# Another order for the first 24 units of a Fourier transform fused with a feed-forward layer

## The chip, the cores and the metric

The kernel runs on one core of a Trainium2 chip. The metric is the device time of one execution in microseconds (us); smaller is better. The core's engines work side by side, each through its own list of instructions in order: TensorE (PE in the profile, with its weight loads as PEld), VectorE (DVE), ScalarE (ACT), GpSimd (POOL) and SyncE (SP), which issues most DMA transfers. An engine waits only where an instruction needs another engine's or a transfer's result, or a buffer that is still in use.

## The reference

```python
X = np.fft.fft(x, axis=1)            # x: 8 batches, 3008 positions, 256 channels
X = np.fft.fft(X, axis=2).real       # 24064 tokens of 256
h = X @ w_in                         # w_in: 256 x 2048
g = np.where(h >= 1, h, np.where(h <= -1, 0.0, (h + 1) ** 2 / 4))
return g @ w_out                     # w_out: 2048 x 256
```

The inputs x are float32; w_in and w_out reach the chip as 64-bit floats, which the kernel converts itself by their bit fields.

## The kernel before

**Tiling.** The transform over 3008 = 64 x 47 positions is made in two stages of matmuls. Stage 1 (PE L276, tiles `s1`) takes sums and differences of mirrored positions, which DVE or POOL folds first (`y`, L132); its results are copied to `z` (ACT L299, DVE L297). Stage 2 (PE L342, tiles `s2`) multiplies z by a constant table `rm` and is split by ACT and DVE into a high and a low part, `pqh` and `pql` (L162, L163). One column, the Nyquist channel, takes a way of its own: a small matmul (L315), a copy, a transfer to memory (`nyr`) and transfers back, spread over all partitions (`nyb`).

The transform over channels is folded into w_in: two constant matrices `cm`, cosine and sine, multiply w_in (PE L251, bank `wps`), and the product is split into `wh` (ACT L252) and `wl` (DVE L262). This is done for four blocks of 512 columns; each block is two folds, one per matrix: `f0 f1`, `f2 f3`, `f4 f5`, `f6 f7`, with `s0` to `s7` as the low parts. Row 0 of the sine product belongs to the Nyquist channel: it is copied to `row` (ACT L255), POOL sets that row of wh and wl to zero (L265), and `spread_delta` turns the row into columns of `delta`, one scalar per partition, with four matmuls of one column each (PE L242) and a copy (ACT L243).

**Units.** The feed-forward part runs in units: one block of 128 of the 2048 hidden columns for one chunk of up to 512 positions. `gemm1` is six matmuls (PE L379, banks `uv`, three of them, two per unit), then on DVE `us` (L382, which reads nyb and delta) and two `h` (L384, L385), and on ACT `a` (L388, L389). `activate` makes `g` on DVE (L397). `gemm2`, the second product, adds g times w_out to four accumulator banks (PE L438); after the last unit of a group the banks are copied out (DVE L449, ACT L447) and stored. There are 384 units. The first twelve take columns 0 to 3 of the first batch's three chunks, the next 36 its other columns, so accumulator groups end with units 3, 7, 11, 23 and so on. Units 0 to 23 use w_out unsplit.

**What sets the order.** For units 0 to 23 the instructions are pinned: each engine works in the order in which the program writes them. Lists of steps, START and STEPS, write the rest of the work between: `l` loads weights, `k` and `m` load constants, `x` loads x, `a`, `b`, `c` and `d` or `v` convert one weight block (fields on DVE L196 and L197; floats on ACT L202 to L204; join on DVE L209 and L210; scale on POOL or DVE L224), `y` folds x, `p` issues matmuls of stage 1, Nyquist or stage 2, `z` and `w` copy stage 1, `t` copies its last column, `q` splits stage 2, `o` splits w_out, `f`, `s` and `e` are the folds above. `p0` to `p7` are stage 1, `p8` the Nyquist matmul, `p9` and on stage 2. In each unit of the loop gemm1 comes first, then activate of the unit before, then the steps, then gemm2 of the unit four before (LAG).

Of the kernel before, what the change touches and what calls it, by code (L numbers as in the profile page):

```python
# [110 lines left out]
def fft_ffn_kernel(ctx: ExitStack, tc: tile.TileContext, x, cst, w_in, w_out, out):  # L111
# [124 lines left out]
    folds, deltas = {}, {}  # L236

    def spread_delta(f4):
# [4 lines left out]
        nc.scalar.activation(delta[:, f4 * 4 : f4 * 4 + 4], pt[:, :4], AF.Copy)  # L243


    def fold_w_in(n):
# [5 lines left out]
        nc.scalar.activation(wh[m][:, cols], pt, AF.Copy)  # L252
        if m == 1:
            row = sb.tile([1, CH], F32, tag="us", name=f"row_{f4}", bufs=2)
            nc.scalar.activation(row, pt[0:1], AF.Copy)  # L255
            deltas[f4] = row
        folds[n] = pt

    def fold_low(n):
# [2 lines left out]
        nc.vector.tensor_tensor(wl[m][:, cols], folds.pop(n), wh[m][:, cols].bitcast(F32), op=ALU.subtract)  # L262
# [349 lines left out]
```

## Time and profile before

| | us |
|---|---|
| median of 3 runs | 1776.84 (1775.87 to 1780.36) |
| the profiled execution's own time | 1775.3 |
| its span, first to last instruction | 1773.5 |
| PE busy | 1743.4 (98%) |
| DVE busy | 1424.8 (80%) |
| ACT busy | 1337.5 (75%) |
| POOL busy | 1162.9 (66%) |
| chain of waits, share of PE | 45% |
| mean granted clock of PE | 0.994 |

PE is busy nearly throughout, so the page as a whole shows little; the first 150 us are the part in which PE has idle time, and there the views by stretch, the waits and the rows in order of time are to be read. A row of the timeline has its start, its duration, the engine, the line, the operation and the count of instructions merged in it; in square brackets stands the idle time ahead of it and who ended it. A matmul of 32-bit floats counts as two instructions.

### The profile page before, as it was taken

The page shows a single profiled execution, that of the slowest core. Times are in us where ns is not written, and L with a number is a line of the kernel's source. Part 1 is how long each engine was busy: PE and PEld are TensorE (multiplying, and loading weights), DVE is VectorE, ACT ScalarE, POOL GpSimd, SP SyncE. Part 2 cuts the span into 40 slices and gives each one's busy share as a digit, 9 for nine tenths or more (in the row PEclk, how much of TensorE's full clock was granted, in tenths as well). Part 3 has the DMA queues.
Part 4 walks back from the last instruction along what each step waited for, and adds up shares of the span by engine and source line. Part 5 has one row for each costly group of instructions (what it writes and reads, how often), then busy time and mean ns, then how long its engine had stood idle before and what let it go on. Part 6 is the DMA issues. An engine that isn't in the chain of part 4 may idle for free.

```text
span 1773.5 us, 21522 instructions
## 1 busy us (share of the span) xinstructions
PE 1743.4 (98%) x7826; PEld 1399.5 (79%) x7826; DVE 1424.8 (80%) x1746; ACT 1337.5 (75%) x1567; POOL 1162.9 (66%) x813
## 2 busy tenths in 40 slices
PE   7889999999999999999999999999999999999998
PEld 5445788888888888888888888888888878888876
DVE  5898787888887888878878878877888778888886
ACT  5676777887777877777777877788778787777775
POOL 0113776876677767677667776677666766667776
PEclk9899999999999999999999999999999999999999
DMA  8003321110011100111001100011000000000000
GB/s 311 23 24 129 130 78 44 41 58 19 24 50 45 60 30 1 60 36 58 30 12 61 59 30 25 16 57 59 30 25 36 1 23 30 13 24 8 16 24 24
DMA packets 32010, 80.88 MB, mean 46 GB/s; under 512 B 2976, under 2 KB 8224, under 8 KB 31904
## 3 DMA queue, kind: packets, MB, share of 16 engines
q1 hardware_dynamic: 31868, 79.51, 12.8%
q8 instruction: 61, 1.00, 0.2%
q14 instruction: 45, 0.37, 0.1%
q10 hardware_dynamic: 36, 0.01, 0.0%
HBM read 51.70 MB, written 27.81 MB: 45 GB/s over the span
## 4 chain that ended last, share of the span: by engine, by line
PE 45%; ACT 21%; DVE 13%; POOL 12%; issue 9%; DMA 0%; ACTq 0%; POOLq 0%; SPq 0%; DVEq 0%
PE acc L438 27%; PE uv L379 13%; POOL gl L406 11%; DVE h L400 9%; ACT a L389 7%; ACT gh L403 6%; ACT a L388 5%; PE s L276 2%; PE s L342 1%; DVE h L384 1%; ACT z L299 1%; DVE h L385 1%; PE wps L251 1%; DVE us L382 0%; DMA raw<-in_moe_w_in_dram 0%
## 5 line engine op out<-in xcount | busy, mean ns | idle before, releaser
L406 POOL TENSOR_TENSOR gl<-h,gh 128x512 fp32r<-128x512 f32 (+1 forms) x720 | 1037.8, 1463 | 438.8 <-ACT gh L403 406.9
L400 DVE SCALAR_TENSOR_TENSOR h<-a,h 128x1024 f32<-128x1024 f32 (+1 forms) x360 | 544.8, 1513 | 219.4 <-ACT a L389 217.9
L403 ACT ACTIVATE gh<-h 128x1024 fp32r<-128x1024 f32 (+1 forms) x360 | 376.2, 1045 | 345.2 <-DVE h L400 318.5
L438 PE MATMUL acc<-gh,woh 128*128 128x512 f32 (+1 forms) x1440 | 570.9, 396 | 3.7 <-DVE o L449 2.2
L438 PE MATMUL acc<-gl,woh 128*128 128x512 f32 (+1 forms) x1440 | 564.4, 392 | 0.9 <-POOL gl L406 0.9
L438 PE MATMUL acc<-gh,wol 128*128 128x512 f32 (+1 forms) x1440 | 561.5, 390 | 0.0
L388 ACT ACTIVATE a<-h,biases 128x1024 f32<-128x1024 f32 (+1 forms) x384 | 431.7, 1124 | 36.4 <-DVE h L385 34.5
L389 ACT ACTIVATE a<-a 128x1024 f32<-128x1024 f32 (+1 forms) x384 | 398.9, 1039 | 7.7
L379 PE MATMUL uv<-pqh,wh 128*128 128x512 f32 (+1 forms) x768 | 311.5, 406 | 11.3 <-DVE us L382 8.3
L438 PEld LDWEIGHTS acc<-gh,woh 128*128 128x128 f32 x1440 | 271.2, 188 | 62.0 <-DVE o L449 5.8
L438 PEld LDWEIGHTS acc<-gl,woh 128*128 128x128 f32 x1440 | 271.5, 189 | 58.3 <-POOL gl L406 2.2
L438 PEld LDWEIGHTS acc<-gh,wol 128*128 128x128 f32 x1440 | 271.1, 188 | 54.2
L384 DVE TENSOR_TENSOR h<-us,uv 128x512 f32<-128x512 f32 (+1 forms) x384 | 259.8, 677 | 61.3 <-POOL gl L406 19.1
L382 DVE SCALAR_TENSOR_TENSOR us<-nyb,delta,uv 128x512 f32<-128x512 f32 (+1 forms) x384 | 279.2, 727 | 30.0 <-PE uv L379 29.8
L379 PE MATMUL uv<-pql,wh 128*128 128x512 f32 (+1 forms) x768 | 300.3, 391 | 0.0
L379 PE MATMUL uv<-pqh,wl 128*128 128x512 f32 (+1 forms) x768 | 300.2, 391 | 0.0
L385 DVE TENSOR_TENSOR h<-us,uv 128x512 f32<-128x512 f32 (+1 forms) x384 | 256.4, 668 | 0.0
L379 PEld LDWEIGHTS uv<-pqh,wh 128*128 128x128 f32 x768 | 144.8, 189 | 57.1 <-DVE us L382 13.8
L379 PEld LDWEIGHTS uv<-pqh,wl 128*128 128x128 f32 x768 | 145.0, 189 | 32.6 <-issue 4.7
L379 PEld LDWEIGHTS uv<-pql,wh 128*128 128x128 f32 x768 | 144.9, 189 | 30.4 <-DVE pql L163 0.4
L132 POOL TENSOR_TENSOR y<-x 96x512 f32<-96x512 f32 x56 | 97.9, 1750 | 2.9 <-PE s L276 2.9
L438 PE MATMUL acc<-g,wo 128*128 128x482 f32 (+1 forms) x192 | 85.2, 585 | 5.1 <-DVE o L449 3.9
(59 smaller groups left out, 707.6 us busy)
## 6 DMA issues: line engine op xcount, KB each, us to landing
x<-in_x_dram SPq DMA_DIRECT2D x64, 512.0 KB, 3.4
out_dram<-o SPq DMA_DIRECT2D x26, 512.0 KB, 2.8
out_dram<-o SPq DMA_DIRECT2D x14, 482.0 KB, 2.9
nyb<-nyr SPq DMA_DIRECT2D x24, 256.0 KB, 3.2
raw<-in_moe_w_in_dram SPq DMA_DIRECT2D x4, 512.0 KB, 8.7
raw<-in_moe_w_out_dram SPq DMA_DIRECT2D x4, 512.0 KB, 10.4
part<-o SPq DMA_DIRECT2D x4, 512.0 KB, 2.6
os<-part SPq DMA_DIRECT2D x4, 512.0 KB, 4.4
```

The source lines that it names most:

```text
L132: (engine or nc.gpsimd).tensor_tensor(y, t[:96, 0], t[:96, 1], op=ALU.add)
L276: nc.tensor.matmul(pt[:, i], y[:, i * P : (i + 1) * P], bm[:96, :], start=True, stop=True)
L379: nc.tensor.matmul(t[:, :n], w[m][:, cols], r[:, m, :n], start=(j == 0), stop=(j == 2))
L382: nc.vector.scalar_tensor_tensor(us, nyb[b, k][:, :n], delta[:, f : f + 1], uv[0], op0=ALU.mult, op1=ALU.add)
L384: nc.vector.tensor_tensor(h[:, 0], us, uv[1], op=ALU.subtract)
L385: nc.vector.tensor_tensor(h[:, 1], us, uv[1], op=ALU.add)
L388: nc.scalar.activation(a, h, AF.Relu, bias=half, scale=0.5)
L389: nc.scalar.activation(a, a, AF.Square)
L400: nc.vector.scalar_tensor_tensor(h, a, 1.0, h, op0=ALU.min, op1=ALU.max)
L403: nc.scalar.activation(gh, h, AF.Copy)
L406: nc.gpsimd.tensor_tensor(gl[:, sg], h[:, sg], gh[:, sg].bitcast(F32), op=ALU.subtract)
L438: nc.tensor.matmul(acc[:, :n], w, g[:, sg], start=(begin and j == 0), stop=(last and j == len(terms) - 1))
```

## The change

The diff, cut to its core; the new functions and the lines that changed in the loop are whole.

```diff
+SKIP = (7, 13)
 START = (
-    "l0 k l1 x0 x1 m0 x2 x3 x4 x5 x6 x7 l2 "
-    "a0 b0 a1 b1 c0 v0 y0 p0 t0 c1 y1 z0 v1 p1 p8 n0 l3 l4 l5 n1 n2 l6 l7 l8 l9 l10 l11 l12 l13 l14 l15 "
-    "y2 z1 f0 y3 p2 p3 z2 y4 s0 p4 w3 f1 y5 p5 w4 y6 p6 s1 w5 y7 p7 w6 e0 w7 p9 p10 q9 q10 a2 b2"
+    "l0 l1 k x0 x1 x2 m0 x3 x4 x5 x6 x7 l2 a0 b0 a1 b1 c0 v0 y0 p0 t0 z0 p8 n0 "
+    "l3 l4 l5 n1 n2 l6 l7 l8 l9 l10 l11 l12 l13 l14 l15 c1 v1 f0 y1 p1 z1 y2 s0 f1 p2 y3 z2 y4 p3 s1 y5 w3 p4 "
+    "y6 w4 p5 y7 w5 p6 w6 p7 e0 w7 E0 p9 p10 q9 q10 a2 b2"
 )
 STEPS = {
-    0: "p11 q11 c2 d2",
-    1: "p12 q12 a3 b3",
+    0: "p11 q11 c2 d2 i5",
+    1: "p12 q12 a3 b3 i5",
...
-    7: "f2 f3 c6 d6 s2 s3 a7 b7",
-    8: "e1 c7 d7",
+    7: "f2 f3 c6 d6 s2 s3 r1 a7 b7",
+    8: "c7 d7",
...
-    17: "o3 L",
-    18: "f6 f7 s6 s7 a14 b14",
-    19: "e3 Y0 c14 d14",
+    17: "o3 L a14 b14",
+    18: "f6 f7 s6 s7 r3",
+    19: "Y0 c14 v14",
...
-EARLY_BANKS = 14
+EARLY_BANKS = 12
...
-    for i, v in enumerate((0.5, 1151.0, 255.0 * 2**23, 1.0)):
+    for i, v in enumerate((0.5, 1151.0, 255.0 * 2**23, 1.0, 1.0)):
...
+    nc.vector.memset(inner[0:1], 0.0)
...
+    def copy_delta(f4):
+        nc.scalar.activation(delta[:, f4 * 4 : f4 * 4 + 4], spreads.pop(f4)[:, :4], AF.Copy)
+
+    def move_delta(f4):
+        row = deltas.pop(f4)
+        for i in range(4):
+            nc.sync.dma_start(
+                delta[:, f4 * 4 + i : f4 * 4 + i + 1], row[:, i * P : (i + 1) * P].rearrange("o (p x) -> o p x", x=1)
+            )
...
-        nc.scalar.activation(wh[m][:, cols], pt, AF.Copy)
+        nc.scalar.activation(wh[m][:, cols], pt, AF.Copy, scale=inner if m else 1.0)
...
-        nc.vector.tensor_tensor(wl[m][:, cols], folds.pop(n), wh[m][:, cols].bitcast(F32), op=ALU.subtract)
+        high = wh[m][:, cols].bitcast(F32)
         if m == 1:
-            for t in (wh[1], wl[1]):
-                nc.gpsimd.memset(t[0:1, cols].bitcast(F32), 0.0)
+            nc.vector.scalar_tensor_tensor(wl[m][:, cols], folds.pop(n), inner, high, op0=ALU.mult, op1=ALU.subtract)
+        else:
+            nc.vector.tensor_tensor(wl[m][:, cols], folds.pop(n), high, op=ALU.subtract)
...
+    def keep_warm(n, src):
+        bank = ps.tile([P, CH], F32, tag="acc3", name="warm_bank", bufs=1)[:, : src.shape[1]]
         for _ in range(n):
-            nc.tensor.matmul(warm_bank[:, :width], warm[:, :P], warm[:, :width], start=True, stop=True)
+            nc.tensor.matmul(bank, src[:, :P], src, start=True, stop=True)
...
+        if 2 <= i < PINNED and i not in SKIP:
+            gemm2(second)
+            second += 1
+        if i < n_units:
             run_steps(STEPS.get(i, ""))
-        if i >= LAG and i < PINNED:
-            gemm2(i - LAG)
```

Steps 13 and 14 change as 7 and 8 do: `r2` in unit 13, no `e2` in unit 14.

**Second product.** It starts in unit 2 and lags two units; none is issued in units 7 and 13, so the lag is three from there and four from unit 14 on, as before. Within a unit it now comes before the steps, so the copies of the accumulators come before the unit's conversions.

**Start.** Both folds of the first block of w_in move ahead of most of stage 1; the second weight load goes ahead of the constants, the load of `cm` behind that of x2; the copy of the first delta (`E0`) goes behind the last copies to z.

**Delta.** The first block keeps its four matmuls. The other three are moved by four transfers each from the row to columns of delta (`r1` to `r3`), in the unit of the fold, and their row takes a buffer of `y`. Row 0 of wh and wl becomes zero by a scalar `inner`, 0 in partition 0 and 1 elsewhere, instead of by POOL's memsets.

**Smaller.** Five matmuls of 128 columns (`i5`) in each of units 0 and 1 write a bank that nobody reads; two of stage 2's banks are no longer those of the accumulators; job 14 is converted one unit earlier and scaled on DVE.

Where rows move, first on PE at the start. Before, from the second stage 1 to the first delta:

```order
L276 MATMUL s_0_1_151<-cs,y_1_144 128x96 x4
L315 MATMUL ny_156<-cs,z_133 24x64
L251 MATMUL wps_194<-cv_114,cm 128x512
L251 MATMUL wps_194<-cv_120,cm 128x512
L276 MATMUL s_0_2_200<-cs,y_2_188 128x96 x4
L276 MATMUL s_0_3_205<-cs,y_3_198 128x96 x4
L276 MATMUL s_0_4_217<-cs,y_4_214 128x96 x4
L251 MATMUL wps_226<-cv_114,cm 128x512
L251 MATMUL wps_226<-cv_120,cm 128x512
L276 MATMUL s_0_5_234<-cs,y_5_232 128x96 x4
```

The changed kernel at the same place:

```order
L327 MATMUL ny_148<-cs,z_135 24x64
L262 MATMUL wps_183<-cv_116,cm 128x512
L262 MATMUL wps_183<-cv_122,cm 128x512
L288 MATMUL s_0_1_189<-cs,y_1_187 128x96 x4
L262 MATMUL wps_201<-cv_116,cm 128x512
L262 MATMUL wps_201<-cv_122,cm 128x512
L288 MATMUL s_0_2_207<-cs,y_2_198 128x96 x4
L288 MATMUL s_0_3_220<-cs,y_3_212 128x96 x4
L288 MATMUL s_0_4_232<-cs,y_4_218 128x96 x4
L288 MATMUL s_0_5_243<-cs,y_5_226 128x96 x4
```

The second fold (the second `wps`) moved from behind five blocks of stage 1 to behind two.

Next DVE in unit 15, where an accumulator group ends. Before, from the unit's `g` to the next unit's `us`:

```order
L397 SCALAR_TENSOR_TENSOR g_831<-a_791,h_788 128x2x482
L209 SCALAR_TENSOR_TENSOR cv_805<-raw_180,cv_805 128x512
L210 SCALAR_TENSOR_TENSOR cv_805<-raw_180,cv_805 128x512
L224 TENSOR_TENSOR cv_805<-cv_805 128x512
L196 TENSOR_SCALAR cv_836<-raw_182 128x512
L197 TENSOR_SCALAR cv_836<-raw_182 128x512
L449 COPY o_0_842<-acc_0_726 128x512
L449 COPY o_1_849<-acc_2_728 128x512
L382 SCALAR_TENSOR_TENSOR us_864<-nyb_0_162,delta,uv_0_856 128x482
```

The changed kernel:

```order
L409 SCALAR_TENSOR_TENSOR g_835<-a_801,h_798 128x2x482
L461 COPY o_0_837<-acc_0_699 128x512
L461 COPY o_1_844<-acc_2_701 128x512
L211 SCALAR_TENSOR_TENSOR cv_813<-raw_172,cv_813 128x512
L212 SCALAR_TENSOR_TENSOR cv_813<-raw_172,cv_813 128x512
L226 TENSOR_TENSOR cv_813<-cv_813 128x512
L198 TENSOR_SCALAR cv_854<-raw_174 128x512
L199 TENSOR_SCALAR cv_854<-raw_174 128x512
L394 SCALAR_TENSOR_TENSOR us_868<-nyb_0_154,delta,uv_0_860 128x482
```

The two copies that free accumulator banks moved ahead of the conversion of two weight blocks.

Last PE around the second block's folds (units 7 and 8). The changed kernel, from the last `uv` rows of unit 7:

```order
L391 MATMUL uv_1_547<-pql_1_317,wh_69 128x512
L262 MATMUL wps_561<-cv_423,cm 128x512
L262 MATMUL wps_561<-cv_463,cm 128x512
L262 MATMUL wps_565<-cv_423,cm 128x512
L262 MATMUL wps_565<-cv_463,cm 128x512
L391 MATMUL uv_0_587<-pqh_2_451,wh_68 128x512
L391 MATMUL uv_0_587<-pqh_2_451,wl_70 128x512
L391 MATMUL uv_0_587<-pql_2_452,wh_68 128x512
L391 MATMUL uv_1_591<-pqh_2_451,wh_69 128x512
```

Before, four rows of the second product of unit 3 (`acc`) stood between the last `wps` and the first of these `uv`; now nothing does.

More of the change, by code (lines that the diff above doesn't have):

```diff
@@ L84 @@
     12: "c10 d10 o0",
-    13: "f4 f5 s4 s5 a11 b11 o1",
-    14: "e2 c11 d11 a12 b12",
+    13: "f4 f5 s4 s5 r2 a11 b11 o1",
+    14: "c11 d11 a12 b12",
     15: "c12 v12 a13 b13",
     16: "c13 v13 o2",
-    17: "o3 L",
-    18: "f6 f7 s6 s7 a14 b14",
-    19: "e3 Y0 c14 d14",
+    17: "o3 L a14 b14",
+    18: "f6 f7 s6 s7 r3",
+    19: "Y0 c14 v14",
     20: "Y1 a15 b15 o4",
@@ L146, in fft_ffn_kernel @@
     delta = wts.tile([P, NFT], F32, name="delta")
-    biases = wts.tile([P, 4], F32, name="biases")
-    for i, v in enumerate((0.5, 1151.0, 255.0 * 2**23, 1.0)):
+    biases = wts.tile([P, 5], F32, name="biases")
+    for i, v in enumerate((0.5, 1151.0, 255.0 * 2**23, 1.0, 1.0)):
         nc.vector.memset(biases[:, i : i + 1], v)
-    half, above, top, one = (biases[:, i : i + 1] for i in range(4))
+    half, above, top, one, inner = (biases[:, i : i + 1] for i in range(5))
+    nc.vector.memset(inner[0:1], 0.0)
     early = [0]
@@ L234, in split_w_out @@
         split(*(wo[t][:, fs].rearrange("p f e -> p (f e)") for t in ("woh", "wol")), wo32[q], nc.gpsimd)
-    folds, deltas = {}, {}
+    folds, deltas, spreads = {}, {}, {}
     def spread_delta(f4):
@@ L242, in spread_delta @@
             nc.tensor.matmul(pt[:, i : i + 1], row[:, i * P : (i + 1) * P], one[0:1], start=True, stop=True)
-        nc.scalar.activation(delta[:, f4 * 4 : f4 * 4 + 4], pt[:, :4], AF.Copy)
+        spreads[f4] = pt
+    def copy_delta(f4):
[6 more added lines that the diff above has]
+            )
     def fold_w_in(n):
@@ L251, in fold_w_in @@
             nc.tensor.matmul(pt, mats[m][h], f32s[4 * f4 + h], start=(h == 0), stop=(h == 1))
-        nc.scalar.activation(wh[m][:, cols], pt, AF.Copy)
+        nc.scalar.activation(wh[m][:, cols], pt, AF.Copy, scale=inner if m else 1.0)
         if m == 1:
-            row = sb.tile([1, CH], F32, tag="us", name=f"row_{f4}", bufs=2)
+            row = sb.tile([1, CH], F32, tag="y" if f4 else "us", name=f"row_{f4}", bufs=3 if f4 else 2)
             nc.scalar.activation(row, pt[0:1], AF.Copy)
@@ L459, in fft_ffn_kernel @@
     nc.gpsimd.memset(warm, 0.0)
-    warm_bank = ps.tile([P, CH], F32, tag="fft", name="warm_bank", bufs=1)
-    def keep_warm(n, width=P):
+    def keep_warm(n, src):
+        bank = ps.tile([P, CH], F32, tag="acc3", name="warm_bank", bufs=1)[:, : src.shape[1]]
         for _ in range(n):
-            nc.tensor.matmul(warm_bank[:, :width], warm[:, :P], warm[:, :width], start=True, stop=True)
-    keep_warm(9, CH)
+            nc.tensor.matmul(bank, src[:, :P], src, start=True, stop=True)
+    keep_warm(9, warm)
     n1 = XC
@@ L499, in fft_ffn_kernel @@
         "e": spread_delta,
-        "i": keep_warm,
+        "E": copy_delta,
+        "r": move_delta,
+        "i": lambda n: keep_warm(n, rm),
         "t": lambda n: stage1_last(0, s1[0, 0]),
@@ L522, in fft_ffn_kernel @@
     pending, done, total = [], 0, 1
+    second = 0
     for i in range(n_units + LAG):
@@ L539, in fft_ffn_kernel @@
                 activate(i)
+        if 2 <= i < PINNED and i not in SKIP:
+            gemm2(second)
+            second += 1
+        if i < n_units:
             run_steps(STEPS.get(i, ""))
-        if i >= LAG and i < PINNED:
-            gemm2(i - LAG)
-        if i < n_units:
             change = units[i][2] == (FIRST if b == 0 else 0) + LAG
@@ L553, in fft_ffn_kernel @@
         if i >= PINNED:
-            gemm2(i - LAG)
+            gemm2(second)
+            second += 1
         if i < PINNED:
```

## The prediction

> **What bounds the kernel now.** I read the stretches first (columns: length; PE, weight load, DVE, ACT and POOL busy with their counts; granted clock; DMA share; GB/s):
>
> ```profile
> 11.35:32.50 21.15, 17.51 (x101) 14.61 (x101) 11.83 (x24) 10.69 (x31) 0.97 (x2) 0.84 0.91 339
> 32.50:56.00 23.50, 15.80 (x56) 10.99 (x57) 18.58 (x31) 14.50 (x19) 2.55 (x2) 0.71 0.39 151
> 56.00:106.00 50.00, 45.23 (x137) 23.84 (x135) 43.67 (x68) 33.73 (x45) 4.03 (x4) 1.00 0.06 20
> 106.00:132.00 26.00, 24.08 (x72) 12.85 (x72) 22.94 (x33) 17.74 (x25) 6.67 (x6) 1.00 0.11 41
> 132.00:152.70 20.70, 20.37 (x63) 11.42 (x64) 17.47 (x23) 12.89 (x18) 5.46 (x6) 1.00 0.50 177
> 152.70:1773.50 1620.80, 1610.67 (x7382) 1321.84 (x7380) 1306.13 (x1559) 1242.76 (x1426) 1141.65 (x787) 1.00 0.11 38
> ```
>
> From 152.7 on, where PE turns to unit 20, it is busy 1610.67 of 1620.80 us, and the change touches nothing there. So the change is worth what it lets PE reach unit 20 earlier. Ahead of that, from 11.35, PE is idle 3.6 + 7.7 + 4.8 + 1.9 + 0.3 = 18.3 us, and its clock is 0.84 and 0.71 in the first two stretches. Next, who waited for whom from 32 to 153 (total, times, longest):
>
> ```profile
> PE uv L379 <- DVE us L382: 8.3, 4, 3.2
> PE acc L438 <- DVE o L449: 3.9, 2, 2.1
> ...
> DVE pql L163 <- ACT pqh L162: 8.9, 5, 2.7
> DVE wl L262 <- ACT wh L252: 3.6, 3, 1.6
> DVE us L382 <- PE uv L379: 2.9, 4, 1.0
> ```
>
> PE waits for DVE; DVE waits for PE only 2.9 us. DVE's larger waits, 8.9 and 3.6, are for ACT copies that stand behind `a` in ACT's queue; both engines keep that order, so they stay. Hence the shorter lag alone buys little: by unit 17 both kernels have the same second products behind them, and DVE sets when. What counts is the start, DVE's own list, and what DVE holds up on PE.
>
> **The start.** Rows by start and duration, of PE, ACT and DVE:
>
> ```profile
> 16.28 2.82 PE L276 MATMUL s<-cs,y 96*128 96x96 f32 x24
> 18.93 1.91 PE L251 MATMUL wps<-cv,cm 128*128 128x512 f32 x4
> ...
> 24.30 1.10 PE L276 MATMUL s<-cs,y 96*128 96x96 f32 x8 [1.69 <-DVE y L132]
> 25.33 1.86 PE L242 MATMUL delta<-biases,row 1*128 1x1 f32 x8
> 28.02 3.79 PE L342 MATMUL s<-cs,z 128*128 128x128 f32 x16 [0.83 <-ACT z L299]
> ...
> 34.20 1.06 PE L342 MATMUL s<-cs,z 128*128 128x128 f32 x8
> ...
> 41.05 0.49 PE L379 MATMUL uv<-pqh,wh 128*128 128x482 f32 x1 [2.93 <-DVE us L382]
> ```
> ```profile
> 21.37 0.57 ACT L255 ACTIVATE row<-wps 1x512 f32<-1x512 f32 x1
> ...
> 27.30 0.67 ACT L299 ACTIVATE z<-s 64x192 f32<-64x192 f32 x2
> ```
> ```profile
> 21.98 0.69 DVE L262 TENSOR_TENSOR wl<-wps,wh 128x512 fp32r<-128x512 f32 x1 [0.91 <-ACT row L255]
> ...
> 23.46 0.69 DVE L132 TENSOR_TENSOR y<-x 96x512 f32<-96x512 f32 x1
> 24.07 0.72 DVE L297 COPY z<-s 64x192 f32<-64x192 f32 x2
> ...
> 33.75 0.71 DVE L382 SCALAR_TENSOR_TENSOR us<-nyb,delta,uv 128x482 f32<-128x482 f32 x1
> ```
>
> The second `wl` stands in DVE's queue ahead of the last folds of x; it waits for the row copy, and PE waits 1.69 us for the y behind it. In the new order both folds of w_in stand right behind the first sums. I walk it with the old durations. The first sum and the Nyquist matmul end near 13.2, the first fold (1.8) at 15.0, one sum (2.65/3 = 0.9, the spacing of the first two rows) at 15.9, the second fold at 17.7. ACT's `wh` and row end at 18.7, the second `wl` at 19.4. Behind it DVE has three y at 0.61 (23.46 to 24.07) and five pairs of z copies at about 0.75 (0.72 and a step): 1.8 + 3.8 = 5.6, so z is whole near 24.9. It was 27.97 (27.30 + 0.67), as ACT's last z copy stood behind the delta copy, which `E0` now puts after it: **3.1 us**. PE then has only short gaps behind it, so I take the full clock: the sixteen matmuls of 3.79 cost 2 x 1.06, **1.7** less. `us` of unit 0 comes near 28.9 instead of 33.75: **4.9 us**. Bounds: 2 (half clock again, and `cm`, now loaded behind x2, a microsecond late) to 6. The ten warm matmuls, 2.6 by the 1.06 for four, lie where PE waited 2.9 and 3.2 us for DVE: nothing; 2.6 without that cover.
>
> **The middle**, on the old clock (the start's gain comes off besides). DVE, one operation by its source line (min/median/max ns), PE, and the chain of waits:
>
> ```profile
> 80.83 0.83 DVE L197 TENSOR_SCALAR cv<-raw_wol 128x512 uint32<-128x512 uint32 x1
> 81.58 1.21 DVE L449 COPY o<-acc 128x482 f32<-128x482 f32 x2
> ...
> 127.42 0.68 DVE L209 SCALAR_TENSOR_TENSOR cv<-raw,cv 128x512 f32<-128x512 uint32 x1
> ...
> 130.02 1.28 DVE L449 COPY o<-acc 128x512 f32<-128x512 f32 x2
> ...
> 140.27 0.72 DVE L382 SCALAR_TENSOR_TENSOR us<-nyb,delta,uv 128x482 f32<-128x482 f32 x1 [0.95 <-PE uv L379]
> ```
> ```profile
> L197 DVE TENSOR_SCALAR cv<-raw_wol x4: 417/421/827, 73.5 to 97.6; 128x512 uint32<-128x512 uint32 x4
> ```
> ```profile
> 130.76 1.08 PE L438 MATMUL acc<-g,wo 128*128 128x482 f32 x2 [1.74 <-DVE o L449]
> 132.33 2.69 PE L438 MATMUL acc<-g,wo 128*128 128x482 f32 x6 [0.50 <-ACT o L447]
> ```
> ```profile
> 139.57 1.31 PE uv L379 x6
> 140.88 3.44 PE wps L251 x8
> 144.32 3.23 PE acc L438 x8
> 147.55 1.31 PE uv L379 x6
> 148.87 0.98 PE delta L242 x8
> ```
>
> - The first eviction moves from unit 7 to unit 5. Its 1.2 us of DVE (81.58) now fill a wait for `pqh`, but ACT's two copies, nearly as long, stand ahead of that `pqh` and delay it 1.0. Sum: 0.2 earlier.
> - POOL's memsets of row 0 fall away. Beside them the `cv` operation took 0.83, its median is 0.42; so in units 7 and 13, 2 x 0.4 = 0.8. The third fold's lies where PE sets the pace: nothing.
> - DVE's waits for `uv`, 2.9 less the last, 0.95, where PE sets the pace: 1.9. Second products now go one unit earlier, and none goes in units 7 and 13, whose folds take 3.44 of PE. I take all of it; bounds 0 and 2.9.
>
> So DVE comes to unit 14 earlier by 0.2 + 0.8 + 1.9 = **2.9**, and keeps that. In unit 15 the two accumulator copies now come ahead of two joins, a multiply and two field operations (127.42 to 130.02): 2.6 more. The extra multiply and fields that come later (units 17 and 19, under 0.7 each) fall where PE sets the pace: nothing, 1.4 otherwise. Allowing 0.2 for the first copy to end, PE's first product on the freed banks moves from 130.76 to about 125.1, **5.7** earlier; the 0.50 behind it goes too, since ACT's copies precede its conversions. Then the delta matmuls of the last fold are gone, **0.98** on the chain (the earlier ones lay under DVE). Against it: in unit 18 the second product now precedes the fold, so the `uv` behind the fold finds its second bank held until `wl` is formed, which waits for ACT's `a` and `wh`: fold and half a `uv` end at 141.4, the bank is free near 142.3, **0.9** lost. Sum 5.7 + 0.5 + 1.0 - 0.9 = **6.3 us**. Bounds 2.5 (the order of the copies alone) and 8.
>
> Delta by transfers: twelve of 512 bytes on SP. The tight ones are the last four: row copied near 142.6, first use at unit 20's `us` near 148.2, 5.6 later, and PE has another 3 us of banks and older products in hand.
>
> ```profile
> nyb<-nyr SPq DMA_DIRECT2D x24, 256.0 KB, 3.2
> ...
> raw<-in_moe_w_out_dram SPq DMA_DIRECT2D x4, 512.0 KB, 10.4
> ```
>
> By the first row they are hidden, by the last (behind other loads) they cost 10.4 - 5.6 - 3 = 1.8. I take 0.
>
> **The clock.**
>
> ```profile
> 42.00:43.00 1.00, 0.62 (x2) 0.55 (x3) 1.00 (x2) 0.58 (x1) 0.00 (x0) 0.70 0.15 57
> ```
>
> It fell right after the wait of 2.93 (this row), and after the 1.69 (the delta matmuls took 1.86 there, 0.98 later); behind the 2.1 of the waits list it stayed at 1.00. A mean of 0.84 over 21.15 us is 6.8 us at half. The new order leaves a gap of its own: with no second product in unit 7, PE stands about 2.2 us in unit 8 until `wl` frees a bank. One spell of 6.8 us at half clock from there costs PE 3.4, of which some 1 is slack ahead of DVE: 2.4. I take half, **1.2**. The Trainium skill, TensorE: Matmul & The Clock Gate, section "What's actually happening", has half rate only after an idle window of some 3.4 us: by it no gap here costs anything and the forecast would be 1765.6. The trace disagrees, as 1.69 was enough, so I keep my term.
>
> **The sum.** 4.9 + 6.3 - 1.2 = **10.0 us**. The profiled execution took 1775.3 (span 1773.5 and 1.8 around it), 1.5 under the median of 1776.84; it would come to 1765.3, the median to **1766.8**.
>
> **Rivals.**
> - *Half clock in units 2 to 5.* With the lag of two, second products stand between one `uv` and the next. In the second stretch PE has 15.80 x 0.71 = 11.2 us of work; three more second products (3.23 each) make it 21 of 23.5 at full clock. One spell of 6.8 us at half leaves 3.4 undone against 2.5 to spare, two leave 6.8: a loss of 1 to 4, and 4 besides the above gives 1770.8. For it: PE will wait some 1.5 us for `g` in unit 3. Against: warm matmuls and earlier products leave no gap like the 2.93. Chance 0.17.
> - *Only the start is kept*: ACT's and DVE's waits for each other re-form in the middle, as with `pqh`. 1776.84 - 4.9 = 1771.9. The 8.9 speaks for it; the rows 130.02 and 130.76, a plain matter of order, against. 0.10.
> - *More*: start 6, middle 8, no half clock: 1763. 0.06.
> - *Slower*: the last four transfers land late and hold `us` of unit 20, behind which all of DVE queues. Each us beyond 8.6 (5.6 + 3) after the row costs one; level with before at 18.6. At 25, 1783. The longer of the two rows above is 10.4, and those are a thousand times larger; 0.04.
> - *Nothing moves*, if another wait ends at the same time throughout: 1776. The idle 18.3 has no such second owner that I see; 0.03.
>
> The forecast keeps 0.60. A difference under 0.3%, 5.3 us, can't be told from no change: faster means under 1771.5. Forecast, "more", two thirds of the first rival and a third of the second make 0.80 faster; same 0.15; slower 0.05. Range 1761 to 1773: above, the first two rivals; below, the upper bounds of the two terms, not quite both at once.
>
> **What would show it.** Right: `us` of unit 0 near 29, clock 1.00 from 25 to 33; the first `acc` row behind unit 15's copies, 130.76 before, near 120; no delta matmul after the first four; PE's first `uv` of unit 20 near 142, and few waits after it. Wrong: a clock of 0.5 from 38 to 50 (first rival); z whole later than 26 (start); `us` of unit 20 waiting for a DMA (slower); or PE waits that have moved past 152.

## The result

The changed kernel takes 1767.8 us (median of 5 runs, 1767.6 to 1769.7), the kernel before, run alternately with it, 1776.7 (1775.9 to 1780.4). The ratio is 0.9949, 95% interval 0.9935 to 0.9964: about 9 us faster. 1766.8 was forecast. The profiled execution took 1767.7 with a span of 1765.9, against 1773.5: 7.6 less in this pair.

The stretches first, cut near the same places of the program as those shown of before (length; PE, weight load, DVE, ACT and POOL busy with their counts; granted clock; DMA share; GB/s):

```profile
11.13:29.59 18.46, 16.48 (x102) 13.42 (x100) 10.01 (x22) 11.02 (x31) 0.00 (x0) 0.91 0.86 313
29.59:52.30 22.71, 19.23 (x85) 13.01 (x86) 17.78 (x30) 13.74 (x17) 2.55 (x2) 1.00 0.53 203
52.30:101.00 48.70, 43.73 (x136) 23.46 (x134) 43.53 (x68) 33.50 (x45) 2.54 (x2) 1.00 0.12 42
101.00:124.00 23.00, 19.49 (x52) 9.77 (x51) 21.23 (x30) 17.00 (x23) 5.70 (x4) 0.93 0.01 0
124.00:144.34 20.34, 19.45 (x56) 10.15 (x56) 17.48 (x27) 13.39 (x19) 6.26 (x5) 1.00 0.45 155
144.34:1765.90 1621.56, 1611.08 (x7382) 1320.04 (x7380) 1307.83 (x1561) 1243.55 (x1426) 1141.96 (x785) 1.00 0.11 38
```

PE turns to unit 20 at 144.34 instead of 152.73, 8.4 us earlier, and behind that it does the same 1611 us of work, in a stretch that is 0.8 longer in this pair (1621.56 after 1620.80). The stretch before unit 5 now runs at full clock (1.00 instead of 0.71). PE still idles before unit 20, but for other things. Who waited for whom from 28 to 146 (total, times, longest), PE and then DVE:

```profile
PE uv L391 <- DVE wl L277: 5.3, 3, 2.4
PE acc L450 <- DVE g L409: 1.9, 2, 1.2
PE s L354 <- DVE pql L165: 1.5, 1, 1.5
...
PE acc L450 <- DVE o L461: 1.4, 2, 1.0
PE uv L391 <- DVE us L394: 0.7, 1, 0.7
```
```profile
DVE pql L165 <- ACT pqh L164: 11.2, 6, 2.7
DVE wl L277 <- ACT wh L263: 3.6, 3, 2.0
```

The wait of `uv` for `us`, 8.3 before, is 0.7; that for the accumulator copies, 3.9 before, is 1.4. New is the wait behind the folds, where the bank is held until `wl` is formed. DVE no longer waits for `uv` in this stretch, but still for ACT, 11.2 and 3.6. DVE is mostly the engine that sets the pace, and the order of its list is the larger part of what the change improved.

The gain has two parts that can be read apart: where `us` of unit 0 starts on DVE (33.75 before, 30.84 now: 2.9), and how long it is from there to PE's first `uv` of unit 20, called **the stretch** below (152.73 - 33.75 = 119.0 before, 144.34 - 30.84 = 113.5 now: 5.5).

### The profile page after: what moved, and what is told of

It reads as the page before. It is cut to its first block, busy times and chain, and to the rows that moved or that the text cites. A ratio compares the mean times of both kernels' runs of the same rounds, so it can differ in the third digit from the quotient of the medians.

```text
span 1765.9 us, 21527 instructions
## 1 busy us (share of the span) xinstructions
PE 1739.3 (98%) x7822; PEld 1394.2 (79%) x7822; DVE 1424.2 (81%) x1749; ACT 1337.3 (76%) x1564; POOL 1160.6 (66%) x804
## 4 chain that ended last, share of the span: by engine, by line
PE 50%; ACT 18%; DVE 12%; POOL 11%; issue 8%; ACTq 0%; POOLq 0%; DVEq 0%
PE acc L450 31%; PE uv L391 15%; POOL gl L418 10%; DVE h L412 7%; ACT a L401 6%; ACT gh L415 5%; ACT a L400 5%; PE s L288 2%; PE s L354 1%; DVE h L396 1%; DVE h L397 1%; ACT z L311 1%; DVE us L394 1%; DVE g L409 1%; PE warm_bank L476 1%
## 5 line engine op out<-in xcount | busy, mean ns | idle before, releaser
L396 DVE TENSOR_TENSOR h<-us,uv 128x512 f32<-128x512 f32 (+1 forms) x384 | 259.6, 676 | 62.4 <-POOL gl L418 19.4
```

The lines of the kernel that those rows point to most:

```text
L396: nc.vector.tensor_tensor(h[:, 0], us, uv[1], op=ALU.subtract)
```

## The experiments

Each ratio is to the kernel before, run beside it on the same chip, with its 95% interval; us of unit 0 and the stretch are from that kernel's trace. None of these kernels leaves out a part of the computation.

| kernel | median, us | ratio | us of unit 0 | stretch |
|---|---|---|---|---|
| before | 1776.7 | 1 | 33.75 | 119.0 |
| changed | 1767.8 | 0.9949 (0.9935 to 0.9964) | 30.84 | 113.5 |
| changed, again | 1769.0 | 0.9948 (0.9935 to 0.9962) | 30.82 | 113.5 |
| 1 new start alone | 1773.0 | 0.9976 (0.9967 to 0.9984) | 30.49 | 119.0 |
| 2 all but the new start | 1771.6 | 0.9972 (0.9961 to 0.9983) | 34.17 | 113.4 |
| 3 copies late again | 1773.6 | 0.9984 (0.9976 to 0.9993) | 30.83 | 119.1 |
| 4 lag of four again | 1769.3 | 0.9959 (0.9947 to 0.9971) | 31.23 | 114.2 |
| 5 order of copies alone | 1774.6 | 0.9979 (0.9970 to 0.9987) | 32.98 | 115.7 |
| 6 delta by matmuls | 1771.0 | 0.9963 (0.9951 to 0.9976) | 33.16 | 116.1 |
| 7 memsets again | 1771.1 | 0.9962 (0.9949 to 0.9974) | 30.92 | 114.3 |
| 8 no warm matmuls | 1770.0 | 0.9959 (0.9947 to 0.9972) | 30.77 | 113.5 |
| 9 delta earlier, warm gap | 1771.3 | 0.9964 (0.9952 to 0.9977) | 32.74 | 115.2 |
| 10 conversions first | 1766.6 | 0.9937 (0.9923 to 0.9951) | 30.36 | 109.9 |
| 11 folds filled | 1763.4 | 0.9916 (0.9904 to 0.9929) | 30.51 | 107.5 |

Medians move by 1 to 2 us from one set of runs to another (the kernel before had 1776.7 to 1779.0), so the ratios and the stretch carry the readings. The stretch is not quite free of the clock either: in kernels 4, 5 and 7 the half clock of the start reaches into unit 0, and `us` of unit 1 comes 6.93 or 6.94 behind that of unit 0 instead of 6.54 or 6.55 in the others up to 9. PE's first `uv` in kernel 4 and in the changed kernel:

```profile
29.62 0.77 PE L391 MATMUL uv<-pqh,wh 128*128 128x482 f32 x1 [0.69 <-ACT pqh L164]
```
```profile
29.59 0.48 PE L391 MATMUL uv<-pqh,wh 128*128 128x482 f32 x1 [0.69 <-ACT pqh L164]
```

Their edits touch nothing that lies so early, so 0.4 of the stretch of these three is not theirs.

**1 and 2: are start and middle separate?** One takes the kernel before with the new START, the other the changed kernel with the old START; nothing else moves (in 2 the copy of the first delta stays right behind its matmuls, as before).

```diff
 # 1, in the kernel before
 START = (
-    "l0 k l1 x0 x1 m0 ... y2 z1 f0 y3 p2 p3 z2 y4 s0 p4 w3 f1 y5 p5 w4 y6 p6 s1 w5 y7 p7 w6 e0 w7 p9 ..."
+    "l0 l1 k x0 x1 x2 m0 ... c1 v1 f0 y1 p1 z1 y2 s0 f1 p2 ... y7 w5 p6 w6 p7 e0 w7 E0 p9 ..."
 # 2, in the changed kernel: the same two lines the other way round
```

> The kernel before with the new START alone: order of loads, both folds of the first block ahead of most of stage 1, the delta copy behind the last copies to z. All else as before. My theory, that the change is a sum of parts that hold by themselves: `us` of unit 0 at 30.8 as in the changed kernel (33.75 before), the clock at half from about 25.8 to 29.3 again, and the time 2.9 less than before, 1773.9. Rival, that the middle takes back what the start gives (DVE and ACT waiting for each other anew): `us` of unit 0 at 30.8, but the time within 1 us of before, 1776 to 1777.

> The changed kernel with the old START. My theory: `us` of unit 0 back near 33.8, the rest as in the changed kernel, 2.9 more than it: 1770.7. Rival, that start and middle are tied (for instance by the clock's windows or by loads that the earlier start outruns): under 1769 or over 1772.

Measured: 4.3 and 5.0 us faster than before (0.0024 and 0.0028 of it), together the change's 9. The traces are plainer still: with the start alone the stretch is 119.0, as before; without it 113.4, as in the changed kernel. The two parts add and don't touch each other; that only the start is kept is ruled out.

**3, 4 and 5: what carries the middle, the lag or the order of the copies?** In 3 the second product stands behind the steps again, lag of two kept; in 4 the lag is four, the order new; 5 is the kernel before with its second product moved ahead of the steps.

```diff
 # 3, in the changed kernel
-        if 2 <= i < PINNED and i not in SKIP:
-            gemm2(second)
-            second += 1
         if i < n_units:
             run_steps(STEPS.get(i, ""))
+        if 2 <= i < PINNED and i not in SKIP:
+            gemm2(second)
+            second += 1
 # 4, in the changed kernel
-        if 2 <= i < PINNED and i not in SKIP:
+        if LAG <= i < PINNED:
 # 5, in the kernel before
+        if i >= LAG and i < PINNED:
+            gemm2(i - LAG)
         run_steps(STEPS.get(i, ""))
-        if i >= LAG and i < PINNED:
-            gemm2(i - LAG)
```

> The changed kernel with the second product behind the unit's steps, as before, and so the accumulator copies behind the conversions; the lag stays two, three, four. My theory: in unit 15 PE's first product on the freed banks comes about 2.6 later and its second wait of 0.5 returns, while in unit 18 the fold goes ahead of the second product again and the 0.9 wait behind it is gone: 3.1 - 0.9 = 2.2 more than the changed kernel, 1770.0. Rival, that the lag pays and the order of copies is hidden: within 0.7 of the changed kernel, 1767 to 1768.5.

> The changed kernel with a lag of four from the start and no unit left out; copies still ahead of conversions. My theory, that the lag itself buys little since DVE sets the pace: the waits of DVE for `uv` (up to 1.9) come back in part, the clock may fall to half in units 2 to 4, where PE has no second product, but PE has spare time there: 1 to 2 more than the changed kernel, 1769 to 1770. Rival, that the shorter lag is what fills PE and carries the middle's gain of 5.5: 1773.3.

> The kernel before with one part of the change alone: the second product, and with it the copies of the accumulators, stands ahead of the unit's steps; the lag stays four, and start, delta and memsets are those of before. Nothing is left out. Theory: the order of the copies carries most of the middle, 2.6 to 2.8 for the first stall and 0.5 for the second, and with the shares of the memsets (0.8) and of the delta matmuls (1.0) taken from the 5.5 measured, up to 3.7: uv of unit 20 at 149.0 to 149.7 instead of 152.73, 3.0 to 3.7 less time than the kernel before, ratio 0.9979 to 0.9983. Rival: the order helps only together with the shorter lag, since DVE comes to unit 14 no sooner; under 1.0 less, ratio over 0.9993.

Measured: without the new order the whole gain of the middle is gone (stretch 119.1), where I had expected a loss of some 2 us. Without the shorter lag 0.7 of it is gone (114.2). With the order alone the stretch falls to 115.7, 3.3 less than before, as expected. Less the 0.4 of the clock, the lag is worth 0.3 and the order alone 3.7, the top of what was expected; the 1 to 2 expected of the lag was too much for the stretch, while the medians (0.0010 above the changed kernel's ratio, with overlapping intervals) can't tell. So the order of the copies is the part that matters, and the shorter lag alone buys little, as the prediction held. It held for the wrong size, though: with the short lag the late copies cost 5.6, more than the 2.6 of a single wait. By `us` of unit 8, 3.0 of it are lost (51.5 behind that of unit 0, 48.5 in the changed kernel), by that of unit 15 no more, and the other 2.6 are lost behind it, where the prediction had put the one wait. PE's waits and a row of PE in kernel 3 show where the first part comes from:

```profile
PE acc L450 <- DVE o L461: 10.7, 3, 4.8
```
```profile
67.81 6.46 PE L450 MATMUL acc<-g,wo 128*128 128x512 f32 x8 [4.84 <-DVE o L461]
```

With a lag of two, PE has the next group's second product in unit 6, right behind the eviction, and stands 4.84 us for the banks; the 6.46 behind it is at half clock. Lag and order are not independent: the short lag brings the eviction into a unit in which DVE's list is long, and needs the copies first there. Kernel 4, with no early second products, has its clock at half from 44 to 54, though the warm matmuls are there (the stretch from 40 to 50):

```profile
40.00:50.00 10.00, 5.17 (x15) 3.17 (x14) 8.11 (x14) 6.67 (x8) 1.27 (x1) 0.69 0.16 61
```

DVE does 8.11 us of work there, as it does in the changed kernel at full clock: the spell is nearly all hidden behind it.

**6 and 7: delta and the memsets.** Each puts one of the two back as before.

```diff
 # 6
-    7: "f2 f3 c6 d6 s2 s3 r1 a7 b7",
-    8: "c7 d7",
+    7: "f2 f3 c6 d6 s2 s3 a7 b7",
+    8: "e1 E1 c7 d7",
 ...   (13 and 14, 18 and 19 likewise)
 # 7
-        nc.scalar.activation(wh[m][:, cols], pt, AF.Copy, scale=inner if m else 1.0)
+        nc.scalar.activation(wh[m][:, cols], pt, AF.Copy, scale=1.0)
 ...
-            nc.vector.scalar_tensor_tensor(wl[m][:, cols], folds.pop(n), inner, high, op0=ALU.mult, op1=ALU.subtract)
+            nc.vector.tensor_tensor(wl[m][:, cols], folds.pop(n), high, op=ALU.subtract)
+            for t in (wh[1], wl[1]):
+                nc.gpsimd.memset(t[0:1, cols].bitcast(F32), 0.0)
```

> The changed kernel with the delta of blocks 2 to 4 by four one-column matmuls and a copy on ACT again (in units 8, 14 and 19, as in the kernel before) instead of by four transfers each. Nothing is left out. Theory: only the last four matmuls lie on the chain, as the prediction had it, and cost 0.98: 1768.8, with uv of unit 20 about 1.0 later than 144.34 and us of units 8 to 14 within 0.3 of the changed kernel's. Rivals: (a) all three sets cost, since with the shorter lag PE is the later engine in units 8 and 14 too: 3 us, 1770.8; (b) none does, since PE has waits behind them that shrink: within 0.4 of 1767.8.

> The changed kernel with row 0 of wh and wl set to zero by POOL's memsets again, instead of by the scalar that is 0 in partition 0. Nothing is left out. Theory: beside the memsets one of DVE's field operations (cv, 0.42 by itself) takes 0.83 again in units 7 and 13, so DVE's us of unit 8 comes 0.4 later than 79.36, that of unit 14 0.8 later than 111.94, and unit 20 0.8 later: 1768.6. Rival: DVE has slack there that the waits for ACT take up (2.7 us at the longest), so us of unit 14 moves by less than 0.3 and the time stays at 1767.8.

Measured for 6: the stretch is 2.6 longer, not 1.0. By unit 10 (`us` of unit 10 is 58.0 behind that of unit 0, 56.9 in the changed kernel) 1.2 are lost, by unit 19 nothing more, and the last set takes 1.5. PE and DVE's waits in kernel 6:

```profile
84.36 1.05 PE L244 MATMUL delta<-biases,row 1*128 1x1 f32 x8
85.34 0.51 PE L391 MATMUL uv<-pqh,wh 128*128 128x512 f32 x1
```
```profile
DVE us L394 <- PE uv L391: 1.1, 2, 0.9
```

In the changed kernel PE is busy without a break from 80 to 100, behind the unit in which it skipped a second product, and DVE is too. There the matmuls of the second block's delta delay `uv`, and DVE waits 1.1 where it waited for nothing. Rival (a) of the expectation was right for two sets of three. The medians agree (0.0014 above the changed kernel's ratio), but their intervals overlap; the trace decides.

Measured for 7: the stretch is 0.8 longer, but it is luck that this is the forecast's number. 0.4 of it is the clock in unit 0. From `us` of unit 7 to that of unit 8 it is 7.72 instead of 7.47, and from unit 13 to unit 14 7.37 instead of 7.11, so the memsets cost 0.25 each time, 0.5 in all (shifts of 0.1 the other way make up the rest). DVE beside POOL, in kernel 7:

```profile
78.99 0.42 DVE L198 TENSOR_SCALAR cv<-raw_wol 128x512 uint32<-128x512 uint32 x1
79.32 0.83 DVE L199 TENSOR_SCALAR cv<-raw_wol 128x512 uint32<-128x512 uint32 x1
```
```profile
79.14 0.73 POOL L277 MEMSET wh<- 1x512 f32 x1 [0.96 <-DVE wl L275]
79.81 0.80 POOL L277 MEMSET wl<- 1x512 f32 x1
```

The field operation of DVE that begins beside a memset on a single partition takes twice its time, 0.4 more; `us`, which begins beside the second memset, takes its usual 0.73. What the forecast left out is the price of the other way: with the scalar, the second low part takes 0.75 instead of 0.69, and it waits 0.35 instead of 0.25 for the row. The ratio of kernel 7 lies 0.0013 above the changed kernel's, 2.3 us, with overlapping intervals; in its profile PE also stands 1.4 us in unit 22, for no reason that the trace names, with a half-clock spell behind, so the medians don't price the memsets and the trace does.

**8: are the warm matmuls needed?**

```diff
-    0: "p11 q11 c2 d2 i5",
-    1: "p12 q12 a3 b3 i5",
+    0: "p11 q11 c2 d2",
+    1: "p12 q12 a3 b3",
```

> The changed kernel without the ten warm matmuls of units 0 and 1 (they write a bank that nobody reads, so nothing is left out of the computation). Theory: they lie in PE's waits for DVE, and earlier second products keep the clock without them, or a half-clock spell there is hidden behind DVE: within 0.5 of the changed kernel beside it, and the stretch from us of unit 0 to uv of unit 20 113.0 to 114.0. Rival (the prediction's first): the clock falls near 37 and stays at half until 48 to 52, and as three more second products now lie there it costs 2 to 4: stretch 115.5 to 117.5.

Measured: the stretch is 113.5, the same; the median is 1.0 above the changed kernel's beside it, with intervals that overlap nearly wholly. The clock from 37 to 53, where the kernel before was at half, in kernel 8:

```profile
37.00:53.00 16.00, 13.23 (x43) 7.31 (x42) 13.88 (x23) 9.91 (x12) 2.56 (x2) 1.00 0.23 88
```

The ten matmuls do nothing here: the early second products are enough to keep the clock up, and PE's waits merely become longer. The prediction's first rival, half clock in units 2 to 5, finds no support with or without them.

**9, and the changed kernel again: why did the clock fall at the start?**

```diff
-    "y6 w4 p5 y7 w5 p6 w6 p7 e0 w7 E0 p9 p10 q9 q10 a2 b2"
+    "y6 w4 p5 e0 y7 w5 p6 w6 p7 i4 w7 E0 p9 p10 q9 q10 a2 b2"
```

> The changed kernel with one edit: the four one-column delta matmuls of the first block stand ahead of the last folds of x, and four warm matmuls of 128 columns (into a bank that nobody reads) stand in front of the sixteen stage-2 matmuls. Nothing is left out of the computation. Theory: the clock fell at about 25.8 us in the changed kernel because the delta matmuls, of one column each, and the gaps around them count as idle for it. With real columns in that gap the clock stays at 1.00 from 24 to 30, the sixteen matmuls take about 2.2 us instead of 3.4, us of unit 0 starts near 29.5 instead of 30.84, and the time falls by 1.2 to 1.4, to about 1766.4. Rival: the clock falls whatever stands there (a fixed spell after the stretch of short waits before); then us of unit 0 stays within 0.3 of 30.84 or comes later by the 1.0 of the four warm matmuls at half clock, and the time is 1767.8 to 1768.8.

> The changed kernel once more, word for word, as the measure for the three kernels beside it and as a second look at its start. Theory: the steps of the granted clock run on a grid of their own, so the half-clock spell at the start begins at another moment than 25.84 and lasts 3.4 or 6.8 us; us of unit 0 lands anywhere from 30 to 33, while the stretch from there to uv of unit 20 repeats to 0.3 of the 113.5 us it took. The ratio to the kernel before is 0.9949 give or take 0.0015. Rival: the spell is set by the program's own gaps and repeats; us of unit 0 is 30.84 within 0.3.

The forecast had full clock for the sixteen matmuls of stage 2. In the changed kernel they took 3.43 us, and the clock fell at 25.84, while PE was busy. The stretches around its two spells:

```profile
22.43:25.84 3.41, 3.08 (x25) 2.80 (x25) 2.79 (x8) 1.51 (x5) 0.00 (x0) 1.00 1.01 391
25.84:29.25 3.41, 3.06 (x15) 2.76 (x14) 0.69 (x1) 0.91 (x2) 0.00 (x0) 0.50 1.01 344
29.25:111.16 81.91, 70.07 (x239) 40.10 (x240) 69.94 (x108) 55.08 (x71) 7.59 (x6) 1.00 0.22 83
111.16:114.57 3.41, 3.41 (x6) 1.35 (x5) 3.31 (x7) 2.81 (x5) 0.18 (x1) 0.50 0.08 1
```

Each spell is 3.41 long, and from the first fall to the second it is 85.32, 25 times 3.413. In the trace of before the falls at 25.34 and 42.40 are 5 times that apart, and the spells 6.83 and 13.65 long, 2 and 4 times. In kernel 9:

```profile
19.21:22.62 3.41, 3.35 (x29) 3.10 (x28) 3.29 (x8) 3.08 (x10) 0.00 (x0) 1.00 0.54 137
22.62:29.45 6.83, 6.72 (x31) 6.46 (x31) 2.73 (x7) 1.53 (x5) 0.00 (x0) 0.50 0.99 375
29.45:80.64 51.19, 42.10 (x167) 25.76 (x167) 40.34 (x64) 32.24 (x42) 3.83 (x3) 1.00 0.29 110
```
```profile
17.69 3.98 PE L288 MATMUL s<-cs,y 96*128 96x96 f32 x32
21.60 1.05 PE L244 MATMUL delta<-biases,row 1*128 1x1 f32 x8
```

My theory failed: the clock fell earlier and for twice as long, right behind a window in which PE was busy 3.35 of 3.41 us, but with matmuls of 96 columns and then of one. So it is not idle time alone that counts there, and warm matmuls put in afterwards, already at half clock, only cost. In the changed kernel the window from 19.02 to 22.43 held less, 2.96 us of busy PE, with matmuls of 96 columns alone, and the clock stayed at full. That matmuls with few columns count for less fits these rows, but no experiment of its own shows it: in kernel 6 the clock fell behind a window of 2.87 us, with matmuls of 96 columns and none of one. The stretch of kernel 9 is 1.7 longer, though its edit ends ahead of unit 0: that is its second spell, in unit 8, and belongs to the clock term below.

From unit 0 to unit 20, where nearly all matmuls have 128 columns or more, the windows between two steps of 3.41 us sort themselves in all fourteen traces. Each fall there ends a window with at most 1.37 us of busy PE, and each window at full clock with 1.55 us or more was followed by full clock.

The grid stands apart from the program. The changed kernel, run again, met nearly the same phase (fall at 25.66, `us` of unit 0 at 30.82), so by itself it shows neither theory. But the warm-up ahead of stage 1 also begins at half clock (in the changed kernel its matmuls start 0.85 us apart at first, and 0.43 apart from 5.55 on), and where it goes over to full clock later, half the delay stays in it: the first sum of stage 1 starts at 11.13 in the changed kernel and anywhere from 10.54 to 11.86 in the others with its start. If both steps are of one grid, the fall must move by twice the difference, give or take whole steps of 3.41. It does, within 0.03, in eight further executions: in kernel 4, first sum at 11.62, the fall should come at 25.84 + 0.98 = 26.82 and came at 26.82; in kernel 6, whose START is the same, first sum at 11.86, at 25.84 + 1.46 - 3.41 = 23.89 and came at 23.88. There the spell took two steps, and `us` of unit 0 came at 33.16, 2.3 later than in the changed kernel. Against the one profile of before, what the start gives is thus 0.6 to 3.4 us from one execution to another. The old START varies too, 32.98, 33.75 and 34.17 in its three profiles (kernels 5, before and 2); the means over these three and over the ten of the new START (30.99) are 2.6 apart, the pair above 2.9.

The Trainium skill, TensorE: Matmul & The Clock Gate, section "What's actually happening", has a free-running window of 3413 ns that the start of a kernel doesn't reset. The traces agree: 25, 5 and 17 steps between falls (kernel 9: 22.62 to 80.64). The same section's idle window as the cause of half rate they don't bear out: the window before a fall held 3.08 and 3.35 us of busy PE.

**10 and 11: is DVE's wait for ACT lost time, and is there a better order?** In 10 DVE converts a weight block before it takes the low part that waits for ACT. 11 does the same, and fills PE's waits behind the folds with the second product.

```diff
 # 10
-    0: "p11 q11 c2 d2 i5",
-    1: "p12 q12 a3 b3 i5",
+    0: "p11 c2 d2 q11 i5",
+    1: "p12 a3 q12 b3 i5",
-    4: "p13 q13 c4 v4 a5 b5",
-    5: "p14 q14 c5 v5",
+    4: "p13 c4 v4 q13 a5 b5",
+    5: "p14 c5 v5 q14",
-    7: "f2 f3 c6 d6 s2 s3 r1 a7 b7",
+    7: "f2 f3 c6 d6 a7 s2 s3 r1 b7",
-    13: "f4 f5 s4 s5 r2 a11 b11 o1",
+    13: "f4 f5 a11 s4 s5 r2 b11 o1",
 # 11, besides
-SKIP = (7, 13)
+SKIP = (8, 14)
+BEHIND = (7, 13, 18)      # here gemm2 stands behind run_steps
-    7: "f2 f3 c6 d6 a7 s2 s3 r1 b7",
+    7: "f2 f3 c6 v6 s2 s3 r1 a7 b7",
```

> The changed kernel with steps reordered inside six units: in units 0, 1, 4 and 5 DVE joins or converts a weight block ahead of the split of stage 2 (pql, which waits for ACT's pqh), and in units 7 and 13 it does the two field operations of a block ahead of the low part wl (which waits for ACT's row and wh). The work is the same, only its order on DVE and ACT moves; nothing is left out. Theory: DVE is the engine that sets when unit 14 comes, and its waits for ACT (11.2 for pqh, 3.6 for wh) are lost time; work of 1.2, 0.7, 1.8, 1.4, 0.7 and 0.7 us, 6.5 in all, now lies in them, of which half to three quarters is kept: uv of unit 20 comes 3 to 5 earlier than 144.34, and the time is 1763 to 1765. Rival: the waits re-form elsewhere, because pql and with it stage 2's banks come later for PE and ACT, or because PE sets the pace by unit 14: within 1.0 of 1767.8, or later.

> A candidate that goes on from the last reorder (conversions ahead of pql in units 0, 1, 4 and 5, and of the low part in unit 13). In it DVE reached unit 8 sooner, and PE's waits for wl behind the folds became 3.4, 2.1 and 0.9. Here the second product stands behind the fold in units 7, 13 and 18, so that it fills these waits, and none is issued in units 8 and 14 instead of 7 and 13; one block is scaled on DVE instead of POOL. Nothing is left out. Theory: 6.4 of PE's idle time is filled, of which DVE's own list lets 1.5 to 2.5 through: the stretch from us of unit 0 to uv of unit 20 is 107.5 to 108.5 (113.5 in the changed kernel, 109.85 with the reorder alone), and the time is 5 to 6 below the changed kernel beside it. Rival: DVE sets the pace throughout, and the filled waits come back one unit later: stretch 109.5 to 110.5, 3 to 4 below. It would be worse, over 111, if the copies of the accumulators came late again behind the steps of unit 13.

Measured for 10: DVE's wait for `pqh` fell from 11.2 to 6.2, the stretch from 113.5 to 109.9: 3.6 of the 6.5 moved were kept. The median, 1766.6, missed the 1763 to 1765 that were expected, and its interval overlaps those of the changed kernel, so this gain is read from the trace alone. PE's waits for `wl` grew, as DVE now reached the folds earlier:

```profile
PE uv L391 <- DVE wl L277: 6.4, 3, 3.4
```

In 11 the eight matmuls of a second product follow the fold of unit 7 with no gap, and PE's wait for `wl` is gone:

```profile
65.03 3.97 PE L263 MATMUL wps<-cv,cm 128*128 128x512 f32 x8
68.84 3.60 PE L451 MATMUL acc<-g,wo 128*128 128x512 f32 x8
71.87 0.80 PE L392 MATMUL uv<-pqh,wh 128*128 128x512 f32 x1
```

The stretch is 107.5, 6.0 shorter than the changed kernel's and within what was expected. The interval of 11, 0.9904 to 0.9929, lies wholly below those of the changed kernel, 0.9935 at the lowest: it beats both kernels, by 5.6 us beside the changed one. That it beats 10 too is not shown by the medians, since their intervals overlap; and of the 2.4 between their stretches a part may be clock alone, as in 10 a half-clock spell begins at 72.42, in unit 8, behind a wait of 3.38 for `wl`, and DVE waits 2.0 for `uv`.

## Why the prediction was right

**The bound.** That PE from unit 20 on is untouched, and that DVE's list sets when unit 20 comes, held: 1611 us behind it in both, and the stretch moved with DVE's list and with what DVE holds up on PE; the delta matmuls of experiment 6, which work on PE, are the exception. That DVE's waits for ACT stay held too: 3.6 and 3.6 for `wl`; for `pqh` 8.9 before, and now 11.2, of which 2.5 is the one in stage 2, ahead of unit 0.

**The start: 4.9 predicted, 2.9 measured; this term was mis-sized.** Its two halves, in PE's and DVE's rows of the changed kernel:

```profile
23.33 1.10 PE L288 MATMUL s<-cs,y 96*128 96x96 f32 x8 [0.27 <-DVE y L133]
24.36 1.05 PE L244 MATMUL delta<-biases,row 1*128 1x1 f32 x8
25.47 3.43 PE L354 MATMUL s<-cs,z 128*128 128x128 f32 x16
```
```profile
18.98 0.75 DVE L275 SCALAR_TENSOR_TENSOR wl<-wps,biases,wh 128x512 fp32r<-128x512 f32 x1 [1.28 <-ACT row L266]
...
23.11 2.22 DVE L309 COPY z<-s 64x192 f32<-64x192 f32 x6
```

The walk put the end of the second `wl` at 19.4 and z whole 5.6 behind it, near 24.9: it was 19.73 and 25.33, the same 5.6. PE's stage 2 came 2.55 earlier (28.02 to 25.47) where 3.1 was taken. The other 1.7, full clock for the sixteen matmuls, failed: 3.43 instead of 3.79, 0.36. The failing step is "PE then has only short gaps behind it, so I take the full clock". The gaps were short, and the clock fell nonetheless, on its grid.

**The middle: 6.3 predicted, 5.5 measured.** Rows of DVE and of PE:

```profile
114.97 1.78 DVE L211 SCALAR_TENSOR_TENSOR cv<-raw,cv 128x512 f32<-128x512 uint32 x1
...
117.61 1.49 DVE L199 TENSOR_SCALAR cv<-raw 128x512 uint32<-128x512 uint32 x1
...
122.04 1.28 DVE L461 COPY o<-acc 128x512 f32<-128x512 f32 x2
```
```profile
77.72 0.50 PE L391 MATMUL uv<-pqh,wh 128*128 128x512 f32 x1 [2.35 <-DVE wl L277]
...
111.07 5.29 PE L450 MATMUL acc<-g,wo 128*128 128x512 f32 x8
...
122.87 3.59 PE L450 MATMUL acc<-g,wo 128*128 128x482 f32 x8 [0.45 <-DVE o L461]
...
140.73 0.48 PE L391 MATMUL uv<-pqh,wh 128*128 128x482 f32 x1 [0.89 <-DVE wl L277]
144.34 0.76 PE L391 MATMUL uv<-pqh,wh 128*128 128x482 f32 x1
```

- DVE at unit 14, measured from `us` of unit 0: 84.0 before, 81.1 now, 2.9 earlier, as forecast. Of its terms, the 0.2 of the first eviction and the 1.9 of the waits for `uv` hold; the memsets' 0.8 is 0.5 (experiment 7), and 0.3 come from shifts of some 0.1 between units that were not forecast.
- Copies ahead of conversions, 2.6 predicted: from `us` of unit 15 to the copies it was 130.02 - 124.40 = 5.62 before and is 122.04 - 119.02 = 3.02 now, 2.6 less.
- "And keeps that" did not quite hold: `us` of unit 15 is only 2.5 earlier (90.65 to 88.18 behind that of unit 0), 0.4 less than that of unit 14. In both kernels POOL operations fall into unit 14 and slow two of DVE's. The second is a field operation, 1.52 before and 1.49 now. The first was `g` before, which took 1.79; now it is the join (L211) beside POOL's split of w_out (L165, 1.81 long from 114.39): 1.78 where its fellow takes 0.68, while `g` takes 1.16. That is 1.1 lost instead of 0.6.
- First product on the freed banks: 5.0 earlier (97.0 to 92.0), 5.7 predicted; the stall behind it is gone (eight matmuls in one row), as predicted.
- Unit 19's bank, 0.9 predicted: 0.89.
- Delta, 0.98 predicted for the last set and nothing for the others: as part of this sum it fits (5.0 + 0.5 + 1.0 - 0.9 = 5.6), yet experiment 6 shows that the transfers are worth 2.6 in the new order. "The earlier ones lay under DVE" was true of the kernel before; in the new one PE has no idle time left from 80 to 100 (busy 20.00 of 20.00 us).
- Transfers of delta hidden: the last four are issued on SP from 141.02, 2.41 us for the four, and no `us` waits for a transfer.

**The clock term: 1.2 predicted; 0 measured in the changed kernel, 1.7 in kernel 9.** The gap foretold in unit 8 was there (2.35, 2.2 foretold), but the clock held. It fell behind the next gap of its kind, unit 13's (2.08), for one step of 3.41; `acc` took 5.29 there instead of 3.60, 1.7 more, and DVE did not wait for it. A spell of 6.8 from unit 8, half counted, was a size and a place that the grid decides. A step of the grid, at 77.03, cuts the gap of unit 8 in two here, and the windows on its two sides held 1.75 and 2.73 us of busy PE; the one that ended at 111.17, with unit 13's gap, held 1.33. In kernel 9 the same gap lies whole in one window, from 77.23 to 80.64, which held 1.06, and the clock fell:

```profile
79.62 0.50 PE L391 MATMUL uv<-pqh,wh 128*128 128x512 f32 x1 [2.35 <-DVE wl L277]
...
80.43 5.29 PE L450 MATMUL acc<-g,wo 128*128 128x512 f32 x8
```
```profile
86.46 0.75 DVE L394 SCALAR_TENSOR_TENSOR us<-nyb,delta,uv 128x512 f32<-128x512 f32 x1 [0.69 <-PE uv L391]
```

There DVE waited for `uv` ahead of this `us` and, 0.88, ahead of the next, and by `us` of unit 10, 1.7 were lost (58.54 behind that of unit 0, 56.85 in the changed kernel), which is all by which that kernel's stretch is longer. So the term named a real cost of the gap, which is 0 or 1.7 in these executions by where the grid lies; that it was 0 in the changed kernel was chance.

So the sum of 10.0 was 8.4 at unit 20 and 9 in the medians: a start too large by 2.0, a middle too large by 0.8, and a clock term too large by 1.2 the other way. The right time owes something to that.

**The rivals.** Half clock in units 2 to 5: 1.00 from 29.59 to 101, with the warm matmuls and, in experiment 8, without. Only the start: experiments 1 and 2. Late delta transfers: no wait for them.

## What to carry to other kernels

Where one engine's list sets the pace ahead of a busy tail, read that engine's waits in order of time and put first what frees another engine's buffers, then work that needs nobody into the waits: here the place of two copies was worth more than a shorter pipeline. A part that is free under the old order (a matmul of one column, a memset beside) can be on the path under the new one, so price it again there. Cost a clock spell as a range of whole steps, not by the length of the gap alone, and don't judge a change of 2 us in the first 30 by one execution. Check a measure for what else it holds before you trust a match: the 0.8 of experiment 7 was half clock and half memsets.
